# Splitting a softmax multiply over two engines and computing two feature blocks together in a kernel's opening

## The chip, the cores and the metric

The kernel runs on one core of a Trainium2 chip. A core has a matrix engine (TensorE, PE in the profile), VectorE (DVE), ScalarE (ACT), GpSimd (POOL) and SyncE (SP, which issues most DMAs). Each engine runs its own list of instructions in order and waits on semaphores for the others. The time is device microseconds of one execution. Before the change it is 418.26 us, the median of three runs (417.74 to 418.84).

## The reference, cut to what matters

Three layers on 4 batches of 576 tokens. The first compresses keys and values of each of 8 heads into 32 memory slots and attends to them; the second picks one of 8 experts per token, the third is a feed-forward layer with a convolution over the tokens:

```python
a   = softmax(phi)                                  # over the tokens' 32 slots
k_m = einsum('bhsm,bhsd->bhmd', a, k)
v_m = einsum('bhsm,bhsd->bhmd', a, v)               # V: 32 slots x 64 per head
s   = (q @ k_m.T) / sqrt(64);  e = exp(s - s.max(-1))
A   = e / (e.sum(-1) + 1e-9)                        # slot weights of each token
x   = A @ v_m                                       # 576 x 512 per batch
h   = relu(x @ w1[e]);  x = p[e] * (h @ w2[e])      # e: a token's expert
h   = relu(x @ w_in);   c = conv3(h) over tokens
out = (h * sigmoid(c)) @ w_out
```

## The kernel before, in words

The kernel never forms `A @ v_m` by itself. It multiplies V by the expert's first weights (V w1, 256 slot rows by 1024 features), and then h = relu(A · V w1), so that the tokens meet a matrix of 256 rows only. Every wide product is taken in a high and a low part, in the format `F32R`: ScalarE copies a float32 tile to its high part, VectorE subtracts that to get the low part, and TensorE runs three products (high·high, high·low, low·high) into one PSUM bank. This is `split` and `matmul3` (lines 145 to 160), and `vw_high` and `vw_low` for V w1.

A batch's tokens are taken in two halves of 288. The names in the profile: `sc` the scores in PSUM, `st` and `sd` the same with tokens down the partitions, `smx` the sums over slots, `at` the weights A with slots down the partitions again, `att` their high and low parts; `pv` the products V w1 in PSUM, `vh` and `vl` their high and low parts; `ph` the products A · V w1, `h` both parts of the relu; `wb` the split second weights w2, `py` the products h w2. `pa` are transposes of `ex`, the exponentials of phi, on TensorE; `nm` is the negative of phi's largest value, `rs` the sums. `idle` are products of the identity that nobody reads (`warm`, line 458).

The order of the work at the start is written by hand. `OPENING` (lines 40 to 48) is a list of steps; with it the order on TensorE, VectorE, ScalarE and SyncE is that of the list, so each of these engines gets its instructions of a step behind those of the step before. What follows the opening is laid out by a planner for TensorE alone, and by a scheduler for the others.

The steps that matter here: `ssum.0.0` (`slot_weights`, line 509) turns the exponentials of batch 0's first half into A; `ahi` and `alo` split it; `vwe`, `vwh`, `vwl` form the first two feature blocks of V w1; `vw.0.1` to `vw.0.3` the other three pairs; each `h.0` is one of eight feature blocks of h. `pmax.3`, `pexp.3` and `prec.3` are the softmax of phi's fourth tile, which `pback.3` transposes on TensorE. `w2part` splits half of the first piece of w2. For the first half alone, `slot_exp`, the sums and the transposes come in two pieces of 9 slot groups (`pieces`, line 483), but the multiply by the reciprocal is one instruction:

```python
nc.vector.tensor_tensor(by_slots(st), d3, of_heads(sm), ALU.mult)      # 128x576
```

Of the kernel before, what the change touches and what calls it, by code (L numbers as in the profile page):

```python
# [14 lines left out]
ALU = mybir.AluOpType  # L15
# [9 lines left out]
HALF = S // 2  # L25
# [15 lines left out]
phi.0 phi.1 kv.0 firstq.0 kv.1 gates phi.2 phi.3 q.0.0 firstq.1 kv.2 warm.0.8  # L41
pmax.0 pexp.0 pmax.1 pexp.1 prec.0 prec.1 pback.0 pback.1 mem.0.0 warm.0.1 mem.0.1 memf.0 warm.0.5 mem.1.0 warm.0.2 mem.1.1 memf.1
frow.0 pmax.2 fexp.0 warm.0.3 back.0 warm.1.2 gatew.0 flog.0 scores.0.0 pexp.2 pback.2
strn.0.0 smx.0.0 ssub.0.0 sexp.0.0 ssum.0.0 warm.1.8 mem.2.0 mem.2.1 warm.1.1 w1.0 q.0.1 wload.0.0 wload.0.1 kv.3 vwe.0 vwh.0 warm.1.2 vwe.1 ahi.0.0 vwh.1 alo.0.0 vwl.0 vwl.1 warm.1.3 wload.0.2
q.1.0 wload.0.3 q.1.1 cload nload.0 nload.1 phi.4 kv.4 prec.2 memf.2 pmax.3
h.0 vw.0.1 h.0 pexp.3 vw.0.2 h.0 prec.3 h.0 w2part.0 vw.0.3 h.0 scores.0.1 strn.0.1 w2part.1 h.0 pback.3 h.0 h.0 smx.0.1 w2.0.1 ssub.0.1 w2.0.2 sexp.0.1
y.0 firstq.2 phi.5 kv.5 mem.3 ssum.0.1 w2.0.3 y.0 back.1 ahi.0.1 alo.0.1 nar.0 nload.2 y.0 gatew.1 frow.1 fexp.1 nar.1 nload.3 y.0
""".split()

# [65 lines left out]
def fused_kernel(tc, q, first, first_q, kv, kv_tail, phi, w1, w2, w_in, conv_w, w_out, out):  # L115
    nc = tc.nc
    wide = w_in.dtype == I64
    PSUM = bass.MemoryType.PSUM
    with (
# [18 lines left out]
        def rows(g):  # L138

            return slice(64 * g, 64 * g + 64)  # L140

        def slots(h):

            return slice(32 * h, 32 * h + 32)
# [2 lines left out]
            pin(nc.scalar.activation(hi, src, AF.Copy))  # L147
            pin((eng or nc.vector).tensor_tensor(lo, src, hi.bitcast(F32), ALU.subtract))  # L148

        def matmul3(outs, pairs, pin=lambda ins: ins, low_last=False):  # L150


            terms = []
            for (sh, sl), (mh, ml) in pairs:
                terms += [(sh, mh), (sh, ml), (sl, mh)]
            if low_last:
                terms = [t for i in range(3) for t in terms[i::3]]
            for i, (st, mv) in enumerate(terms):
                for ps, cols in outs:
                    pin(nc.tensor.matmul(ps, st, mv[:, cols], start=i == 0, stop=i == len(terms) - 1))  # L160

        def urgent():

            return tc.high_priority(offset=1500)
# [7 lines left out]
        def half(i):  # L172
            return slice(i * HALF, (i + 1) * HALF)
# [336 lines left out]
        def slot_weights(b, hf):  # L510
            st, d3 = sts.pop((b, hf)), by_slots(sds.pop((b, hf)))
            sm = ap.tile([128, 18], F32, tag="smx", bufs=2, name=f"smx{b}_{hf}")
            for hs in pieces(b, hf):
                nc.vector.reduce_sum(sm[:, hs], d3[:, hs], axis=AX.X)
            nc.vector.tensor_scalar(sm, sm, EPS, None, ALU.add)
            nc.vector.reciprocal(sm, sm)
            nc.vector.tensor_tensor(by_slots(st), d3, of_heads(sm), ALU.mult)
            attf[b, hf] = ap.tile([128, 2, HALF], F32, tag="at", bufs=4, name=f"at{b}_{hf}")
            for hs in pieces(b, hf):
                cols = slice(32 * hs.start, 32 * hs.stop)  # L520
                nc.vector.transpose(attf[b, hf].rearrange("p g t -> p (g t)")[:, cols], st[:, cols])
# [6 lines left out]
        def slot_softmax(b, hf):  # L528

            slot_top(b, hf)  # L530
            slot_exp(b, hf)
            slot_weights(b, hf)
# [183 lines left out]
        att, e0 = {}, {}  # L716
# [10 lines left out]
        def vw_product(vs, raws, q, name, into=None):  # L727


            hi, lo = into or (fps[-1].tile([128, 4, 2, 128], F32R, tag="vw", bufs=4, name=f"{p}{name}_{q // 2}")  # L730
                              for p in ("vh", "vl"))
            ps = banks(f"pv{name}_{q}")
            at = q % 2
            for i, raw in enumerate(raws):
                fs = slice(2 * (at + i), 2 * (at + i) + 2)
                by_head(by_block(ps)[:, :, fs], lambda g, h: vs[rows(g), slots(h)], lambda g, h: by_block_head(raw)[rows(g), :, h])
            with urgent():
                fs = slice(2 * at, 2 * (at + len(raws)))
                vw_high(hi, ps, fs)
                vw_low(lo, hi, ps, fs)  # L740
            return hi, lo

        def by_block(ps):
            return ps.rearrange("p g (f n) -> p g f n", f=4)

        def by_block_head(raw):
            return raw.rearrange("p (f h n) -> p f h n", f=2, h=4)

        def vw_high(hi, ps, fs):
            nc.scalar.activation(hi[:, fs], ps.rearrange("p g (f n) -> p f g n", f=4)[:, fs], AF.Copy)  # L750

        def vw_low(lo, hi, ps, fs):
            nc.vector.tensor_tensor(lo[:, fs], ps.rearrange("p g (f n) -> p f g n", f=4)[:, fs],
                                    hi[:, fs].bitcast(F32), ALU.subtract)
# [17 lines left out]
        def hidden(vw, at, f, hf, name):  # L772

            ps = bank(f"ph{name}_{hf}{f}")[:, :HALF]
            hi, lo = vw[f // 4]
            matmul3([(ps, half(hf))],
                    [((hi[:, f % 4, g, :], lo[:, f % 4, g, :]), (at[:, g, 0, :], at[:, g, 1, :])) for g in range(2)],
                    low_last=f"{name}{hf}{f}" == "000")
            t = fps[-1].tile([128, 2, HALF], F32R, tag="h", bufs=8, name=f"h{name}_{hf}{f}")
            with urgent():  # L780
                nc.scalar.activation(t[:, 0, :], ps, AF.Relu)  # L781
                low = nc.vector.scalar_tensor_tensor(t[:, 1, :], ps, 0.0, t[:, 0, :].bitcast(F32), ALU.max, ALU.subtract)  # L782
                hidden_low.append(low.ins)
            return t

        def second(hs, wbb, d, name):
            ps = bank(f"py{name}_{d}")[:, :HALF]
            w = wbb[d].rearrange("p s (f d) -> p s f d", f=8)
            matmul3([(ps, slice(0, HALF))],
                    [((w[:, 0, f], w[:, 1, f]), (hs[f][:, 0, :], hs[f][:, 1, :])) for f in range(8)])  # L790
            return ps
# [14 lines left out]
        late, wbs, vws, wi, hids, count = [], {}, {}, {}, [], {}  # L806
# [93 lines left out]
        def load_first():  # L900
            ys0.append(load_y(0, expert(0)))

        def split_first():
            ys0.append(y_parts(0))
            split_y(0, ys0[0], *ys0[1])

        def gated_w(kc):
# [7 lines left out]
            "scores": scores, "gatew": gate_weights, "firstq": first_queries, "frow": first_row, "fexp": first_weights, "flog": first_expert, "ssoft": slot_softmax,  # L915
            "pmax": phi_max, "pexp": phi_exp, "prec": phi_sums, "smax": slot_top, "strn": scores_back, "smx": slot_max,
            "ssub": slot_difference, "sexp": slot_exp, "ssum": slot_weights, "ahi": attention_high, "alo": attention_low,
            "rtok": route_tokens, "save": save, "rback": route_back, "rall": route_all, "rpp": route_scan, "rown": route_first, "asplit": split_attention,
            "vwe": first_vw, "vwh": first_vw_high, "vwl": first_vw_low, "vw": expert_vw, "w2": expert_w2, "nload": load_words, "nar": narrow, "win": gated_w,
            "conv": conv_weights, "cload": load_conv, "w1": expert_w1, "w2part": first_w2, "wload": load_w2, "close": close, "yload": lambda b: load_first(), "ysplit": lambda b: split_first(), "h": next_hidden, "y": next_second,  # L920
        }

# [27 lines left out]
        def other_experts(b):  # L950
# [8 lines left out]
            with tc.For_i(0, E) as e:  # L959
                fl = nc.values_load(fli[0:1, ds(b * E + e, 1)], min_val=0, max_val=1)  # L960
                with tc.If(fl > 0):
# [188 lines left out]
```

## Time and profile before

The profiled execution took 417.01 us, 1.25 us less than the median above. Its span, from the first to the last instruction that the profile shows, is 415.2 us, so 1.8 us lie outside it.

| Engine | busy us | share of the span | instructions |
| --- | --- | --- | --- |
| PE (matmul) | 406.6 | 98% | 3406 |
| DVE | 276.3 | 67% | 509 |
| ACT | 222.0 | 53% | 414 |
| POOL | 74.6 | 18% | 121 |

The times of instructions are taken from the span's start. Busy time of TensorE includes the `idle` products, and a busy matrix engine is not one at its peak. The mean granted clock of the matrix engine was 0.997 of full speed. What the change touches lies between 16 and 32 us of the span.

### The profile page before, as it was taken

Reading aid. Unit: us, or ns where it says so; the run is one execution under the profiler, and the core shown is the slowest. Engines: PE = TensorE matmul, PEld = TensorE weight load, DVE = VectorE, ACT = ScalarE, POOL = GpSimd, SP = SyncE. Lnnn points to the kernel's source line nnn. Section 1 sums busy time; section 2 is a strip of 40 time slices with the busy share of each in tenths; the row PEclk is TensorE's granted clock in tenths of the full one; section 3 lists DMA queues with packets and bytes.
Section 4 is the critical chain, followed back from the end, with each engine's and each line's share of the span. In section 5 each row is a group of like instructions: output and inputs, shape, how many; then the busy total and the mean of one; then the engine's idle time right before and its main releaser. Section 6 shows DMA issues by size and latency. Waiting matters only on the chain.

```text
span 415.2 us, 8514 instructions
## 1 busy us (share of the span) xinstructions
PE 406.6 (98%) x3406; PEld 370.6 (89%) x3407; DVE 276.3 (67%) x509; ACT 222.0 (53%) x414; POOL 74.6 (18%) x121
## 2 busy tenths in 40 slices
PE   8999999999999999999999999999999999999994
PEld 7779988989989998899999988998889988999884
DVE  3689899695777974966979980688105792178500
ACT  4366577455657264645848742677215772277320
POOL 1000202311122211311101620034100332014300
PEclk9999999999999999999999999999999999999998
DMA  8999989967892699946640032000120000100022
GB/s 288 343 403 401 340 305 363 410 220 277 303 310 93 200 366 407 340 157 186 194 152 0 2 114 103 0 2 0 57 70 2 0 2 29 72 2 2 2 77 57
DMA packets 23904, 69.04 MB, mean 166 GB/s; under 512 B 3280, under 2 KB 4048, under 8 KB 23856
## 3 DMA queue, kind: packets, MB, share of 16 engines
q1 hardware_dynamic: 20272, 56.88, 39.1%
q0 software_dynamic: 3584, 11.54, 7.1%
q8 instruction: 28, 0.46, 0.5%
q14 instruction: 20, 0.16, 0.1%
HBM read 52.08 MB, written 16.33 MB: 165 GB/s over the span
## 4 chain that ended last, share of the span: by engine, by line
PE 96%; ACT 1%; DMA 1%; DVE 1%; issue 0%; ACTq 0%
PE py L160 25%; PE pi L160 24%; PE po L1058 24%; PE ph L160 12%; PE pv L455 2%; PE pk L412 2%; PE idle L462 2%; PE sc L455 1%; PE pa L390 1%; DMA ph<-in_phi 1%; PE pl L593 1%; PE pk L402 0%; DVE wb L148 0%; PE pkt L446 0%; ACT wb L147 0%
## 5 line engine op out<-in xcount | busy, mean ns | idle before, releaser
L160 PE MATMUL py<-h,wb 128*128 128x288 f32 x768 | 108.2, 298 | 0.0
L160 PEld LDWEIGHTS py<-h,wb 128*128 128x128 f32 x768 | 103.0, 188 | 4.2 <-issue 3.4
L160 PE MATMUL pi<-yh,wi 128*128 128x288 f32 x512 | 90.4, 295 | 0.0
L1058 PE MATMUL po<-wo,g 128*128 128x512 f32 (+1 forms) x408 | 90.2, 377 | 0.0
L1058 PEld LDWEIGHTS po<-wo,g 128*128 128x128 f32 x408 | 72.8, 188 | 13.2
L160 PEld LDWEIGHTS pi<-yh,wi 128*128 128x128 f32 x512 | 76.3, 188 | 0.9
L1040 DVE SCALAR_TENSOR_TENSOR ct<-ht,convw,ct 128x575 f32<-128x575 f32 x32 | 31.0, 968 | 52.1 <-ACT ct L1039 52.1
L160 PE MATMUL pi<-yl,wi 128*128 128x288 f32 x256 | 54.6, 295 | 0.0
L160 PE MATMUL ph<-att,vh 128*128 128x288 f32 x256 | 53.5, 302 | 0.3 <-DVE h L782 0.3
L1023 POOL CAST tail<-g 128x128 fp32r<-128x128 f32 x32 | 23.0, 723 | 122.9 <-DVE g L148 122.3
L160 PEld LDWEIGHTS ph<-att,vh 128*128 128x128 f32 x256 | 40.6, 188 | 4.6 <-DVE h L782 1.7
L865 POOL DMA_DIRECT2D ydram<-ys x32 | 17.4, 545 | 146.7 <-ACT ys L864 140.3
L160 PEld LDWEIGHTS pi<-yl,wi 128*128 128x128 f32 x256 | 41.1, 188 | 0.0
L1037 ACT ACTIVATE ht<-pi 128x576 f32<-128x576 f32 x32 | 20.8, 651 | 33.5 <-PE pi L160 33.5
L160 PE MATMUL ph<-att,vl 128*128 128x288 f32 x128 | 37.7, 296 | 0.0
L782 DVE SCALAR_TENSOR_TENSOR h<-ph,h 128x288 fp32r<-128x288 f32 x64 | 28.1, 449 | 12.8 <-ACT h L781 12.7
L781 ACT ACTIVATE h<-ph 128x288 fp32r<-128x288 f32 x64 | 25.7, 408 | 16.5 <-PE ph L160 16.1
L864 ACT ACTIVATE ys<-py 128x288 f32<-128x288 f32 x32 | 13.1, 408 | 37.5 <-PE py L160 25.2
L1082 ACT ACTIVATE ot<-po 128x512 f32<-128x512 f32 x17 | 9.5, 598 | 43.3 <-PE po L1058 43.3
L1018 DVE TENSOR_TENSOR ct<-ht,ct 128x576 f32<-128x576 f32 x32 | 27.0, 844 | 7.2 <-ACT ct L1017 7.1
L1042 DVE SCALAR_TENSOR_TENSOR ct<-ht,convw,ct 128x575 f32<-128x575 f32 x32 | 28.3, 886 | 0.4
L147 ACT ACTIVATE g<-ct 128x576 fp32r<-128x576 f32 x32 | 21.7, 681 | 12.6 <-DVE ct L1018 12.6
(234 smaller groups left out, 505.2 us busy)
## 6 DMA issues: line engine op xcount, KB each, us to landing
kv<-in_kv SPq DMA_DIRECT2D x16, 512.0 KB, 8.5
q<-in_q SPq DMA_DIRECT2D x8, 576.0 KB, 10.3
ydram<-ys POOLq DMA_DIRECT2D x32, 144.0 KB, 5.3
y<-ydram SPq DMA_DIRECT2D x4, 1152.0 KB, 6.8
out<-ot SPq DMA_DIRECT2D x15, 256.0 KB, 2.0
ph<-in_phi SPq DMA_DIRECT2D x8, 288.0 KB, 7.3
adram<-at POOLq DMA_DIRECT2D x8, 288.0 KB, 7.7
wa_1r<-in_w SPq DMA_DIRECT2D x4, 512.0 KB, 4.5
```

Source lines behind the costliest of these rows:

```text
L147: pin(nc.scalar.activation(hi, src, AF.Copy))
L160: pin(nc.tensor.matmul(ps, st, mv[:, cols], start=i == 0, stop=i == len(terms) - 1))
L781: nc.scalar.activation(t[:, 0, :], ps, AF.Relu)
L782: low = nc.vector.scalar_tensor_tensor(t[:, 1, :], ps, 0.0, t[:, 0, :].bitcast(F32), ALU.max, ALU.subtract)
L864: nc.scalar.activation(yt, ps, AF.Copy)
L865: stored.append(nc.gpsimd.dma_start(ydram[b, d, :, half(hf)], yt).ins)
L1018: slow(f"gm.{f}").tensor_tensor(ct, ht, ct, ALU.mult)
L1023: nc.gpsimd.tensor_copy(tail[:, f, :, to:to + 64], t[:, :, 512:576].bitcast(F32))
L1037: nc.scalar.activation(two(ht), halves(ps), AF.Relu)
L1040: nc.vector.scalar_tensor_tensor(ct[:, 1:], ht[:, :S - 1], convw[:, 0, f:f + 1], ct[:, 1:], ALU.mult, ALU.add)
L1042: nc.vector.scalar_tensor_tensor(ct[:, :S - 1], ht[:, 1:], convw[:, 2, f:f + 1], ct[:, :S - 1], ALU.mult, ALU.add)
L1058: nc.tensor.matmul(ps[:, cols], st[sp], w[:, mp, f % 2, cols], start=f == 0 and i == 0, stop=f == 7 and i == 2)
```

## The change: what it does

- The multiply in `slot_weights` of the first half becomes two of 128x288. GpSimd takes the second (slot groups 9 to 17), VectorE the first.
- Of the 14 `idle` products between `pa` of phi's third tile and h, 8 stay: 5 behind `pa` and 3 between the two feature blocks of `pv_0`.
- The first two feature blocks of h are computed together. `hp` issues the eight products with the high part of V w1 for both, `hq` behind `vw.0.1` the four with the low part and then both relus. Before, block 0 stood ahead of `vw.0.1` (with its low products last, by `low_last`) and block 1 behind it.
- The split of `vw.0.1` into high and low parts is done in two pieces of 128x256.
- `pmax.3` and `pexp.3` move from in front of the first `h.0` and from behind the second to behind the fourth, ahead of `w2part.0`; `prec.3` moves from behind the third `h.0` to behind the fifth.

```diff
-strn.0.0 smx.0.0 ssub.0.0 sexp.0.0 ssum.0.0 warm.1.8 mem.2.0 mem.2.1 warm.1.1 w1.0 ... vwe.0 vwh.0 warm.1.2 vwe.1 ahi.0.0 vwh.1 alo.0.0 vwl.0 vwl.1 warm.1.3 wload.0.2
-q.1.0 wload.0.3 q.1.1 cload nload.0 nload.1 phi.4 kv.4 prec.2 memf.2 pmax.3
-h.0 vw.0.1 h.0 pexp.3 vw.0.2 h.0 prec.3 h.0 w2part.0 vw.0.3 h.0 scores.0.1 strn.0.1 w2part.1 h.0 pback.3 h.0 h.0 ...
+strn.0.0 smx.0.0 ssub.0.0 sexp.0.0 ssum.0.0 warm.1.5 mem.2.0 mem.2.1 w1.0 ... vwe.0 vwh.0 warm.1.3 vwe.1 ahi.0.0 vwh.1 alo.0.0 vwl.0 vwl.1 wload.0.2
+q.1.0 wload.0.3 q.1.1 cload nload.0 nload.1 phi.4 kv.4
+hp.0 prec.2 memf.2 vw.0.1 hq.0 h.0 vw.0.2 h.0 pmax.3 pexp.3 w2part.0 vw.0.3 h.0 prec.3 scores.0.1 strn.0.1 w2part.1 h.0 pback.3 h.0 h.0 ...
...
-            nc.vector.tensor_tensor(by_slots(st), d3, of_heads(sm), ALU.mult)
             attf[b, hf] = ap.tile([128, 2, HALF], F32, tag="at", bufs=4, name=f"at{b}_{hf}")
+            for hs in pieces(b, hf)[::-1]:
+                (nc.gpsimd if 0 < hs.start else nc.vector).tensor_tensor(
+                    by_slots(st)[:, hs], d3[:, hs], of_heads(sm[:, hs]), ALU.mult)
...
                 fs = slice(2 * at, 2 * (at + len(raws)))
-                vw_high(hi, ps, fs)
-                vw_low(lo, hi, ps, fs)
+                for part in [slice(f, f + 1) for f in (2, 3)] if (name, q) == ("0", 1) else [fs]:
+                    vw_high(hi, ps, part)
+                for part in [slice(f, f + 1) for f in (2, 3)] if (name, q) == ("0", 1) else [fs]:
+                    vw_low(lo, hi, ps, part)
...
+        def first_hidden(low):
...
+            for i, (st, mv) in enumerate([(1, 0)] if low else [(0, 0), (0, 1)]):
+                for f in range(2):
+                    for g in range(2):
+                        nc.tensor.matmul(first_ps[f], vw[st][:, f, g, :], at[:, g, mv, :HALF],
+                                         start=not low and i == g == 0, stop=low and g == 1)
+            if low:
+                count["h"] = 1
+                hids.extend(hidden_out(first_ps[f], f, 0, "0") for f in range(2))
```

`hidden_out` holds the two instructions of the relu (lines 781 and 782 of before) that stood in `hidden`.

On TensorE, from the last `idle` products to `pv_2` (`att` is A split, the number behind a name tells tiles apart). Before:

```order
L462 MATMUL idle_275<-ident 128x128 x2
L455 MATMUL pv_0_394<-wa_0r,vt_273 32x128 x8
L462 MATMUL idle_275<-ident 128x128 x3
L160 MATMUL ph_00_454<-att_414,vh_0_392 128x288 x4
L160 MATMUL ph_00_454<-att_414,vl_0_393 128x288 x2
L455 MATMUL pv_1_464<-wa_1r,vt_273 32x256 x8
L160 MATMUL ph_01_475<-att_414,vh_0_392 128x288 x2
L160 MATMUL ph_01_475<-att_414,vl_0_393 128x288
L160 MATMUL ph_01_475<-att_414,vh_0_392 128x288 x2
L160 MATMUL ph_01_475<-att_414,vl_0_393 128x288
L455 MATMUL pv_2_490<-wa_2r,vt_273 32x256 x8
```

And now:

```order
L460 MATMUL idle_275<-ident 128x128 x3
L453 MATMUL pv_0_391<-wa_0r,vt_273 32x128 x8
L798 MATMUL ph_00_440<-att_412,vh_0_389 128x288 x2
L798 MATMUL ph_01_441<-att_412,vh_0_389 128x288 x2
L798 MATMUL ph_00_440<-att_412,vh_0_389 128x288 x2
L798 MATMUL ph_01_441<-att_412,vh_0_389 128x288 x2
L453 MATMUL pv_1_457<-wa_1r,vt_273 32x256 x8
L798 MATMUL ph_00_440<-att_412,vl_0_390 128x288 x2
L798 MATMUL ph_01_441<-att_412,vl_0_390 128x288 x2
L158 MATMUL ph_02_480<-att_412,vh_0_389 128x288 x2
```

The products with `vl` of blocks 0 and 1 now stand behind `pv_1`, and three `idle` products in front of `ph_00` are gone.

On ScalarE, from the split of `pv_1` to the relu of block 4 (`h_04`); `ex` from `ph_143` is `pexp.3`, the half piece of `wb_0` is `w2part.0`. Before:

```order
L750 ACTIVATE vh_0_392<-pv_1_464 128x512
L781 ACTIVATE h_01_482<-ph_01_475 128x288
L369 ACTIVATE ex_485,rs_486<-ph_143,nm_452 128x576
L750 ACTIVATE vh_1_488<-pv_2_490 128x512
L781 ACTIVATE h_02_508<-ph_02_501 128x288
L781 ACTIVATE h_03_522<-ph_03_515 128x288
L147 ACTIVATE wb_0_525<-wb_0r 128x512
L750 ACTIVATE vh_1_488<-pv_3_528 128x512
L781 ACTIVATE h_04_546<-ph_04_539 128x288
```

And now:

```order
L752 ACTIVATE vh_0_389<-pv_1_457 128x256 x2
L785 ACTIVATE h_00_474<-ph_00_440 128x288
L785 ACTIVATE h_01_477<-ph_01_441 128x288
L785 ACTIVATE h_02_487<-ph_02_480 128x288
L752 ACTIVATE vh_1_490<-pv_2_492 128x512
L785 ACTIVATE h_03_510<-ph_03_503 128x288
L367 ACTIVATE ex_515,rs_516<-ph_143,nm_513 128x576
L147 ACTIVATE wb_0_518<-wb_0r 128x512
L752 ACTIVATE vh_1_490<-pv_3_521 128x512
L785 ACTIVATE h_04_539<-ph_04_532 128x288
```

The exponential went from in front of block 2's relu (`h_02`) to between block 3's (`h_03`) and `wb_0`.

On VectorE, over the same steps (`nm` is `pmax.3`, `rs` with `nm`'s `ex` is `prec.3`). Before:

```order
L364 TENSOR_REDUCE nm_452<-ph_143 128x1
L782 SCALAR_TENSOR_TENSOR h_00_461<-ph_00_454,h_00_461 128x288
L753 TENSOR_TENSOR vl_0_393<-pv_1_464,vh_0_392 128x512
L782 SCALAR_TENSOR_TENSOR h_01_482<-ph_01_475,h_01_482 128x288
L753 TENSOR_TENSOR vl_1_489<-pv_2_490,vh_1_488 128x512
L782 SCALAR_TENSOR_TENSOR h_02_508<-ph_02_501,h_02_508 128x288
L372 TENSOR_SCALAR rs_486<-rs_486 128x1
L373 RECIPROCAL rs_486<-rs_486 128x1
L375 TENSOR_SCALAR rs_513<-rs_486 128x1
L782 SCALAR_TENSOR_TENSOR h_03_522<-ph_03_515,h_03_522 128x288
L148 TENSOR_TENSOR wb_0_525<-wb_0r,wb_0_525 128x512
L753 TENSOR_TENSOR vl_1_489<-pv_3_528,vh_1_488 128x512
L782 SCALAR_TENSOR_TENSOR h_04_546<-ph_04_539,h_04_546 128x288
```

And now:

```order
L755 TENSOR_TENSOR vl_0_390<-pv_1_457,vh_0_389 128x256 x2
L786 SCALAR_TENSOR_TENSOR h_00_474<-ph_00_440,h_00_474 128x288
L786 SCALAR_TENSOR_TENSOR h_01_477<-ph_01_441,h_01_477 128x288
L786 SCALAR_TENSOR_TENSOR h_02_487<-ph_02_480,h_02_487 128x288
L755 TENSOR_TENSOR vl_1_491<-pv_2_492,vh_1_490 128x512
L786 SCALAR_TENSOR_TENSOR h_03_510<-ph_03_503,h_03_510 128x288
L362 TENSOR_REDUCE nm_513<-ph_143 128x1
L148 TENSOR_TENSOR wb_0_518<-wb_0r,wb_0_518 128x512
L755 TENSOR_TENSOR vl_1_491<-pv_3_521,vh_1_490 128x512
L786 SCALAR_TENSOR_TENSOR h_04_539<-ph_04_532,h_04_539 128x288
```

The reduction of `ph_143`, which `ex` needs, now stands behind the low part of block 3 and in front of `wb_0` and the last `vl`.

On TensorE nothing changes place from block 2 to `py`. The new kernel's rows from the second half's scores (`sc_1`) to block 6 (`ph_06`), with the engine that an instruction waits for:

```order
L453 MATMUL sc_1_546<-q_1_380,vt_273 32x288 [waits DMAHW5_49,PE_49]
L453 MATMUL sc_1_546<-q_1_380,vt_273 32x288 x7
L158 MATMUL ph_05_559<-att_412,vh_1_490 128x288 x2
L158 MATMUL ph_05_559<-att_412,vl_1_491 128x288
L158 MATMUL ph_05_559<-att_412,vh_1_490 128x288 x2
L158 MATMUL ph_05_559<-att_412,vl_1_491 128x288
L388 MATMUL pa_569<-ident,ex_515 128x128 [waits DVE_49]
L388 MATMUL pa_569<-ident,ex_515 128x128 x3
L390 MATMUL pa_569<-ident,ex_515 128x128
L158 MATMUL ph_06_578<-att_412,vh_1_490 128x288 [waits Activation_49]
L158 MATMUL ph_06_578<-att_412,vh_1_490 128x288
```

Here the transposes `pa` stand behind block 5 in both kernels, and their first instruction waits for VectorE: for the last `vl`, which empties the PSUM banks of `pv_3` that `pa` takes over.

## Rows read from the trace of the kernel before

**Rows 1.** Page part 4: the chain that ended last, shares by engine.

```profile
PE 96%; ACT 1%; DMA 1%; DVE 1%; issue 0%; ACTq 0%
```

**Rows 2.** Chain of waits, 16 to 34 us: start us, us, what.

```profile
16.48 1.79 PE idle L462 x16
...
19.62 0.42 PE idle L462 x2
...
20.42 0.64 PE idle L462 x4
...
21.44 0.86 PE idle L462 x6
22.31 1.05 PE ph L160 x6
23.36 0.59 PE pv L455 x16
23.95 0.98 PE ph L160 x6
...
25.52 1.91 PE ph L160 x12
```

**Rows 3.** VectorE in order of time: start, us, line, out<-in [idle before].

```profile
19.53 0.27 DVE L516 RECIPROCAL smx<-smx 128x18 f32<-128x18 f32 x1
19.83 0.76 DVE L517 TENSOR_TENSOR st<-sd,smx 128x576 f32<-128x576 f32 x1
20.62 0.84 DVE L521 STREAM_TRANSPOSE at<-st 128x288 f32<-128x288 f32 x2
...
22.35 0.75 DVE L753 TENSOR_TENSOR vl<-pv,vh 128x256 fp32r<-128x256 f32 x2
...
23.58 0.28 DVE L435 SCALAR_TENSOR_TENSOR q0r<-pk,rs,q0r 128x64 f32<-128x64 f32 x1
...
23.79 0.75 DVE L364 TENSOR_REDUCE nm<-ph 128x1 f32<-128x576 f32 x1
...
28.07 0.45 DVE L782 SCALAR_TENSOR_TENSOR h<-ph,h 128x288 fp32r<-128x288 f32 x1
29.07 0.69 DVE L148 TENSOR_TENSOR wb<-wb_0r,wb 128x512 fp32r<-128x512 f32 x1 [0.55 <-ACT wb L147]
29.68 0.68 DVE L753 TENSOR_TENSOR vl<-pv,vh 128x512 fp32r<-128x512 f32 x1
```

**Rows 4.** ScalarE in order of time, the same stretch.

```profile
21.84 0.36 ACT L750 ACTIVATE vh<-pv 128x256 fp32r<-128x256 f32 x1
23.91 0.37 ACT L437 ACTIVATE pm<-pk,rs 128x128 f32<-128x128 f32 x1 [1.70 <-DVE q0r L435]
...
25.27 0.77 ACT L369 ACTIVATE ex<-ph,nm 128x576 f32<-128x576 f32 x1
...
27.47 0.41 ACT L781 ACTIVATE h<-ph 128x288 fp32r<-128x288 f32 x1 [0.38 <-PE ph L160]
28.41 0.63 ACT L147 ACTIVATE wb<-wb_0r 128x512 fp32r<-128x512 f32 x1 [0.53 <-DMA wb_0r<-in_w]
28.94 0.58 ACT L750 ACTIVATE vh<-pv 128x512 fp32r<-128x512 f32 x1
```

**Rows 5.** TensorE in order of time: the transposes of ex.3.

```profile
30.48 0.60 PE L390 MATMUL pa<-ident,ex 128*128 128x128 f32 x4
```

**Rows 6.** VectorE in order of time, 241 to 245 us.

```profile
241.52 0.81 DVE L1040 SCALAR_TENSOR_TENSOR ct<-ht,convw,ct 128x575 f32<-128x575 f32 x1
242.37 2.07 DVE L1042 SCALAR_TENSOR_TENSOR ct<-ht,convw,ct 128x575 f32<-128x575 f32 x1
```

**Rows 7.** GpSimd in order of time, the same stretch.

```profile
242.40 1.42 POOL L148 TENSOR_TENSOR g<-ct,g 128x576 fp32r<-128x576 f32 x1 [4.23 <-ACT g L147]
```

**Rows 8.** Stretches: us, busy us of each engine (instructions), PEclk, DMA, GB/s.

```profile
174.00:175.20 1.20, 0.86 (x7) 0.62 (x6) 1.20 (x5) 0.79 (x2) 0.00 (x0) 1.00 1.00 409
...
409.00:415.20 6.20, 0.23 (x2) 0.03 (x1) 0.00 (x0) 0.38 (x1) 0.00 (x0) 0.79 0.09 29
```

More of the change, by code (lines that the diff above doesn't have):

```diff
@@ L43 @@
 frow.0 pmax.2 fexp.0 warm.0.3 back.0 warm.1.2 gatew.0 flog.0 scores.0.0 pexp.2 pback.2
-strn.0.0 smx.0.0 ssub.0.0 sexp.0.0 ssum.0.0 warm.1.8 mem.2.0 mem.2.1 warm.1.1 w1.0 q.0.1 wload.0.0 wload.0.1 kv.3 vwe.0 vwh.0 warm.1.2 vwe.1 ahi.0.0 vwh.1 alo.0.0 vwl.0 vwl.1 warm.1.3 wload.0.2
-q.1.0 wload.0.3 q.1.1 cload nload.0 nload.1 phi.4 kv.4 prec.2 memf.2 pmax.3
-h.0 vw.0.1 h.0 pexp.3 vw.0.2 h.0 prec.3 h.0 w2part.0 vw.0.3 h.0 scores.0.1 strn.0.1 w2part.1 h.0 pback.3 h.0 h.0 smx.0.1 w2.0.1 ssub.0.1 w2.0.2 sexp.0.1
+strn.0.0 smx.0.0 ssub.0.0 sexp.0.0 ssum.0.0 warm.1.5 mem.2.0 mem.2.1 w1.0 q.0.1 wload.0.0 wload.0.1 kv.3 vwe.0 vwh.0 warm.1.3 vwe.1 ahi.0.0 vwh.1 alo.0.0 vwl.0 vwl.1 wload.0.2
+q.1.0 wload.0.3 q.1.1 cload nload.0 nload.1 phi.4 kv.4
+hp.0 prec.2 memf.2 vw.0.1 hq.0 h.0 vw.0.2 h.0 pmax.3 pexp.3 w2part.0 vw.0.3 h.0 prec.3 scores.0.1 strn.0.1 w2part.1 h.0 pback.3 h.0 h.0 smx.0.1 w2.0.1 ssub.0.1 w2.0.2 sexp.0.1
 y.0 firstq.2 phi.5 kv.5 mem.3 ssum.0.1 w2.0.3 y.0 back.1 ahi.0.1 alo.0.1 nar.0 nload.2 y.0 gatew.1 frow.1 fexp.1 nar.1 nload.3 y.0
@@ L148, in split, with matmul3 @@
             pin((eng or nc.vector).tensor_tensor(lo, src, hi.bitcast(F32), ALU.subtract))
-        def matmul3(outs, pairs, pin=lambda ins: ins, low_last=False):
+        def matmul3(outs, pairs, pin=lambda ins: ins):
             terms = []
@@ L155, in matmul3 @@
                 terms += [(sh, mh), (sh, ml), (sl, mh)]
-            if low_last:
-                terms = [t for i in range(3) for t in terms[i::3]]
             for i, (st, mv) in enumerate(terms):
@@ L776, in hidden, with hidden_out @@
             matmul3([(ps, half(hf))],
-                    [((hi[:, f % 4, g, :], lo[:, f % 4, g, :]), (at[:, g, 0, :], at[:, g, 1, :])) for g in range(2)],
-                    low_last=f"{name}{hf}{f}" == "000")
+                    [((hi[:, f % 4, g, :], lo[:, f % 4, g, :]), (at[:, g, 0, :], at[:, g, 1, :])) for g in range(2)])
+            return hidden_out(ps, f, hf, name)
+        def hidden_out(ps, f, hf, name):
             t = fps[-1].tile([128, 2, HALF], F32R, tag="h", bufs=8, name=f"h{name}_{hf}{f}")
@@ L784, in hidden @@
             return t
+        def first_hidden(low):
+            vw, at = vws[0][0], att[0]
+            if not low:
+                first_ps.extend(bank(f"ph0_0{f}")[:, :HALF] for f in range(2))
+            for i, (st, mv) in enumerate([(1, 0)] if low else [(0, 0), (0, 1)]):
[6 more added lines that the diff above has]
+                hids.extend(hidden_out(first_ps[f], f, 0, "0") for f in range(2))
+        first_ps = []
         def second(hs, wbb, d, name):
@@ L918, in fused_kernel @@
             "rtok": route_tokens, "save": save, "rback": route_back, "rall": route_all, "rpp": route_scan, "rown": route_first, "asplit": split_attention,
-            "vwe": first_vw, "vwh": first_vw_high, "vwl": first_vw_low, "vw": expert_vw, "w2": expert_w2, "nload": load_words, "nar": narrow, "win": gated_w,
+            "hp": lambda b: first_hidden(False), "hq": lambda b: first_hidden(True), "vwe": first_vw, "vwh": first_vw_high, "vwl": first_vw_low, "vw": expert_vw, "w2": expert_w2, "nload": load_words, "nar": narrow, "win": gated_w,
             "conv": conv_weights, "cload": load_conv, "w1": expert_w1, "w2part": first_w2, "wload": load_w2, "close": close, "yload": lambda b: load_first(), "ysplit": lambda b: split_first(), "h": next_hidden, "y": next_second,
```

## The prediction, made before the changed kernel ran

> **What bounds the kernel now.** I read the shares of the chain that ended last first. TensorE holds 96% of it and no other engine more than 1% [rows 1], so a change counts only by what it does to TensorE's own row of work: products taken out of it, or gaps put in. Next I read the chain between 16 and 34 us, where everything moved lies [rows 2]. It never leaves TensorE there. But four of its pieces are `idle` products, which stand where the engine would otherwise wait: 1.79 + 0.42 + 0.64 + 0.86 = 3.71 us. So the stretch before h is bound by what the idle products cover, the making of A on VectorE and ScalarE. Then come the three lists of instructions in order of time. VectorE works without a gap from the reciprocal at 19.53 to 23.8 [rows 3]; ScalarE waits for its results [rows 4]. Behind them TensorE runs densely to `pa` at 30.48 [rows 5], which waits for VectorE's last `vl`. That `vl` ran from 29.68 to 30.36 [rows 3], so it is ready about when TensorE arrives, with no slack to spend. Work of block 3 of h ends on TensorE at T = 25.52 + 1.91 = 27.43 [rows 2]; from there to `pa` it has 30.48 − 27.43 = 3.05 us of work (`pv_3`, block 4, scores, block 5). The change leaves that list alone.
>
> **Part 1: fewer idle products.** Fourteen become eight (each has two records). At the old rates 5 of the first 8 take 1.12 us and 3 of the last kind 0.86, 1.98 in all, so 1.73 us of products go. I cost this at nothing: they covered waits for A's high part and for `vh`, whose times don't hang on them. TensorE just waits instead.
>
> **Part 2: the multiply split over two engines.** Now it takes 0.76 us, 19.83 to 20.59, and the transposes start at 20.62 [rows 3]. If nothing collided, VectorE's half would take 0.38, and GpSimd's second half 0.71 to 0.75, half of the 1.42 that a 128x576 multiply took there [rows 7]; the second transpose could go about 0.4 us earlier. But both engines read the same two tiles at the same time, and at 242 us the trace has such a pair. A GpSimd multiply ran 242.40 to 243.82, its normal 1.42 [rows 7], and the VectorE instruction of 242.37 beside it took 2.07 us, where its twin just before took 0.81 [rows 6]. It ended at 244.44, 0.62 behind GpSimd: VectorE stood still and then did most of its work. The same here: the reciprocal ends at 19.80, GpSimd works 19.87 to 20.62, and VectorE's half ends 0.38 × 0.62 / 0.81 = 0.29 later, at 20.91. The transposes start at 20.93 in place of 20.62: **+0.31 us** for all that hangs on A. The ends for GpSimd's half are 0.71 (no cost per instruction) and 1.42 (all of it), so the term lies between −0.4, without a collision, and +1.0. I take +0.31, from the one pair of rows that shows both engines on such work.
>
> The Trainium skill ("SBUF — State Buffer", section "SBUF: two separate sides") has a rule for such a pair: the two engines share a port pair as an exclusive lock, and whichever starts first holds it for its whole instruction. The trace agrees that one stands still (2.07 against 0.81 us), but there the engine that lost had started 0.03 us before the other. By the rule VectorE, which starts at 19.83, goes first and GpSimd follows to about 20.95; the multiply would then cost the second transpose little, which is the second case below.
>
> **Part 3: two blocks of h together, the split of `vw.0.1` in two.** The first of these products needs A's high part and `vh`. The second `vh` ends at 21.84 + 0.36 = 22.20 [rows 4], and by +0.31 at 22.51. TensorE issues block 1's high products from 22.56; the six products from there take 0.98, as six do between two `pv` [rows 2], to 23.54. `pv_1` takes 0.59 [rows 2], to 24.13, and the four low ones 4 × 0.16 = 0.64 (12 products took 1.91 [rows 2]), to 24.77. Here something new is late. Block 2 needs `vw.0.1` split. ScalarE must first do `pm`, which waits for `q0r`: 23.58 + 0.28 + 0.31 = 24.17, so `pm` runs 24.22 to 24.59 [rows 3, 4]. Then come two `vh` of 0.36 with about 0.28 between their starts, 24.51 to 25.15. VectorE's first `vl` waits for both, 25.18 to 25.59 (half of the pair's 0.75 and the overlap [rows 3]). Block 2's third product takes that `vl` at 25.62; its last four products end at 26.26. `pv_2` 0.59, block 3 0.98: T = 27.83, against 27.43. **+0.40 us** at the end of block 3, 0.09 of it from the new order itself. Block 0 no longer waits for the first `vl` pair ahead of `pv_1`; this wait stands in its place.
>
> **Part 4: `pmax.3` and `pexp.3` moved behind block 3.** This is where I see most of the cost. Before, the reduction ran at 23.79 and `ex` at 25.27 [rows 3, 4], while TensorE was busy elsewhere, and ScalarE idled 0.53 us for `wb_0r` from memory ahead of its 28.41 [rows 4]. Now both stand in the chain that `pa` waits for. In order: block 3 ends at T; relu on ScalarE T+0.04, 0.41 [rows 4], ends T+0.45; low part on VectorE 0.03 later, 0.45 [rows 3], ends T+0.93; `nm` 0.08 before that end (instructions overlap so much in these rows), 0.75 [rows 3], ends T+1.60; `ex` 0.05 later, 0.77 [rows 4], ends T+2.42; `wb_0`'s high part 0.63 [rows 4] to T+3.05, with `wb_0r` long there; its low part starts T+3.08, the last `vl` 0.61 behind it (29.07 to 29.68), 0.68 [rows 3], ends T+4.37; `pa` some 0.03 later, at T+4.40. TensorE arrives at T+3.05. A new wait of **1.35 us**, where before there was almost none. `prec.3` is moved behind the low part of block 4, and nobody waits for it (its user, `pm` of the fourth tile, comes after `pa`).
>
> **Sum.** `pa` starts 0.40 + 1.35 = 1.75 us later. From `pa` on TensorE has dense work of the same order in both kernels, so this passes to the end: 417.01 + 1.75 = 418.76 against the profiled execution of 417.01, and 418.26 + 1.75 = **420.0 us** against the median. The removed products return none of it.
>
> **Rivals.**
> - *VectorE goes first in the multiply.* Against: the rows of part 2. For: it is ready 0.04 to 0.07 earlier than I put GpSimd's start. Then part 2 costs near nothing and T shifts by 0.09: 0.09 + 1.35 = 1.44, 419.7 us. By the Trainium skill's rule of part 2 this is what happens.
> - *The transfer of `wb_0r` already delays `pa` in the runs that are timed.* The median lies 1.25 us above the profiled execution, and in that one ScalarE already waited for this transfer [rows 4]. If it lands 1 us later than 28.41 there, the old kernel stalls at `pa` by about as much, and the new one, which needs it only at T+2.42 = 30.25, does not. The cost is then 1.75 less about 1: 418.9 us. Against: nothing says that the 1.25 us lie here.
> - *Not slower: VectorE's last `vl` doesn't hold `pa`.* One place and one price: if the chain behind block 3 is done by T+3.05, as when the reduction and `ex` start on their own inputs instead of behind block 3's relu, part 4 is free. `nm` would have to run 1.35 us earlier, in VectorE's gaps at block 2. With A's transposes 0.4 us earlier (part 2 without a collision) the time falls by about 0.6 at most, 417.7 us. Against: each engine takes its instructions in the list's order, and the list has the reduction behind block 3's low part.
> - *The clock.* The row of 409 to 415 us shows a granted clock of 0.79 behind a TensorE that had almost stopped (0.23 us busy of 6.20), and at 174 us a gap of 0.34 in 1.20 left it at 1.00 [rows 8]. If a wait of 1.35 us at `pa` dropped it from 2.4 to 1.2 GHz, the next products run at half speed: the 12 of blocks 6 and 7 take 1.91 us now [rows 2] and would take that much more, with as many of `py` 3.8 us, so 422 to 424 us. The gap is nearer to 174's, so I give it little.
>
> **How the numbers follow.** My forecast 0.42, VectorE first 0.24, the late transfer 0.20, not slower 0.09, the clock 0.05. The two first together give 419.7 to 420.0; with the bounds of part 2 (T from −0.25 to +1.1) they reach from 1.1 to 2.5 us over the median, 419.4 to 420.8. The range of 8 in 10 takes in the late transfer downward and a little of the clock upward: 418.2 to 421.3. What this kernel's measurement tells from no change is about 0.3%, 1.25 us. Slower by more: most of the forecast (0.38), half of VectorE first (0.13), the clock (0.05): 0.56. Within: the late transfer (0.19), the rest of those two (0.15), half of not slower: 0.38. Faster by more: 0.06, if part 2's full gain and no wait at `pa` come together.
>
> **What would show it.** Right: in the profile after, `pa` of the fourth tile starts near 32.2 and 1.3 us behind the last product of block 5, with the wait put down to `vl`; `ex` runs just ahead of `wb_0` near 29.5; GpSimd's multiply takes about 0.75 and VectorE's half beside it about 1.0; the first transpose starts near 20.9. Wrong: `pa` within 0.3 us of block 5's end; a VectorE half of 0.4 us; a gap in front of block 2 well over 0.7 us or none; a PEclk under 1.00 behind `pa`. If the time is under 418, the transfer or the order of the engines was not what I read.

## The result and the profile after

The changed kernel took 420.82 us, the median of 21 runs (419.30 to 424.15), against 418.69 us of the kernel before, measured anew beside it (21 runs, 417.74 to 420.82). The ratio is 1.0058 with an interval of [1.0041, 1.0074]: slower by 0.6%, where I forecast 420.0 us in 418.2 to 421.3. The profiled execution took 421.19 us, its span 419.4.

The page's shares of the chain that ended last, now:

```profile
PE 90%; DMA 3%; DVE 3%; ACT 2%; issue 0%; SPq 0%; POOL 0%; ACTq 0%; POOLq 0%
```

Against [rows 1] TensorE gave up 6 points to transfers, VectorE and ScalarE: the chain now leaves it. The points of the transfers aren't the change's own: these pieces are a `kv` at the start and one at 62 to 69 us, both told below. The chain of waits from block 3 of h to `pa` (start us, us, what):

```profile
27.50 1.00 PE ph L158 x6
28.52 0.42 ACT h L785
...
28.97 0.46 DVE h L786
29.42 0.67 DVE nm L362
...
30.12 0.87 ACT ex L367 x2
30.99 0.53 ACT wb L147
...
31.55 0.69 DVE wb L148
32.24 0.61 DVE vl L755
32.85 0.04 issue
32.89 0.66 PE pa L388 x4
```

It is the chain that the prediction built link by link. Block 3 ends at 28.48 (its last product 28.19 + 0.29), `pa` starts at 32.89, so 4.41 us later; forecast were 4.40. In [rows 2, 5] this was 3.05. TensorE in order of time says how long it stood:

```profile
31.39 0.30 PE L158 MATMUL ph<-att,vl 128*128 128x288 f32 x1
32.89 0.66 PE L388 MATMUL pa<-ident,ex 128*128 128x128 f32 x4 [1.20 <-DVE vl L755]
```

The bracket is the wait and who ended it: 1.20 us for the last `vl`. Where there is no wait an instruction starts about 0.16 before its predecessor's end, so `pa` came 1.36 us late (4.41 − 3.05).

The multiply of A. VectorE and GpSimd in order of time:

```profile
20.43 0.27 DVE L514 RECIPROCAL smx<-smx 128x18 f32<-128x18 f32 x1
20.73 0.46 DVE L517 TENSOR_TENSOR st<-sd,smx 128x288 f32<-128x288 f32 x1
21.23 1.01 DVE L521 STREAM_TRANSPOSE at<-st 128x288 f32<-128x288 f32 x2
```

```profile
20.85 0.87 POOL L517 TENSOR_TENSOR st<-sd,smx 128x288 f32<-128x288 f32 x1 [18.80 <-DVE smx L514]
```

VectorE went first and was not held up: 0.46 us, not 1.0. The second transpose waits for GpSimd and ends 1.54 us behind the reciprocal (22.24 − 20.70), where before both ended 1.66 behind it ([rows 3]: 21.46 − 19.80). The split saves 0.12 us.

Two more pieces of the 4.2 us between the two spans lie outside all this. The reciprocal itself came 0.90 us later than in [rows 3], a shift from before anything that the change touches: the second `kv` landed at 9.00 us and TensorE waited for it.

```profile
9.05 0.65 PE L410 MATMUL pk<-kv,a 128*32 128x128 f32 x16 [0.85 <-DMA kv<-in_kv]
```

And at 69 us ScalarE waited for the next expert's `wb_0r`, with TensorE behind it:

```profile
68.27 1.06 ACT L147 ACTIVATE wb<-wb_0r 128x1024 fp32r<-128x1024 f32 x1 [2.10 <-DMA wb_0r<-in_w]
```

```profile
70.77 0.26 PE L453 MATMUL pw<-wgl,vt 64*32 64x9 f32 x13 [1.61 <-ACT vt L446]
```

So of 4.2 us, 0.90 is a late `kv`, 0.15 the front of the change (block 3 ends 7.79 behind the reciprocal, before 7.64), 1.36 the wait at `pa`, 1.61 a late transfer at 69 us; 0.2 lie in smaller pieces. Whether the two transfers belong to the change only more kernels could say.

### The profile page after: what moved, and what is told of

Same layout as the page of the kernel before. It is cut to its first block, busy times and chain, and to the rows that moved or that the text cites. A ratio compares the mean times of both kernels' runs of the same rounds, so it can differ in the third digit from the quotient of the medians.

```text
span 419.4 us, 8495 instructions
## 1 busy us (share of the span) xinstructions
PE 406.2 (97%) x3394; PEld 369.0 (88%) x3395; DVE 276.2 (66%) x510; ACT 222.1 (53%) x415; POOL 75.6 (18%) x122
## 4 chain that ended last, share of the span: by engine, by line
PE 90%; DMA 3%; DVE 3%; ACT 2%; issue 0%; SPq 0%; POOL 0%; ACTq 0%; POOLq 0%
PE pi L158 24%; PE py L158 24%; PE po L1078 23%; PE ph L158 11%; DMA q<-in_q 2%; DMA kv<-in_kv 2%; PE pv L453 2%; PE pk L410 2%; PE sc L453 1%; PE idle L460 1%; PE pa L388 1%; PE pl L593 1%; DVE wb L148 0%; DVE vl L755 0%; PE pk L400 0%; ACT wb L147 0%
## 5 line engine op out<-in xcount | busy, mean ns | idle before, releaser
L158 PE MATMUL ph<-att,vh 128*128 128x288 f32 x248 | 52.0, 302 | 0.3 <-DVE h L786 0.3
L158 PEld LDWEIGHTS ph<-att,vh 128*128 128x128 f32 x248 | 39.3, 188 | 4.5 <-DVE h L786 1.9
L158 PE MATMUL ph<-att,vl 128*128 128x288 f32 x124 | 36.6, 295 | 0.2 <-DVE vl L755 0.2
```

## The experiments

All kernels that follow are read by the same four marks, taken from the reciprocal of the slot sums (R) so that a late transfer at the start doesn't count: R itself, the end of block 3 behind R, the start of `pa` behind block 3, and the rest of the span (spans are known to 0.1 us). The ratio is that of the times to the kernel before on the same chip.

| kernel | R | block 3 − R | pa − block 3 | span − pa | ratio [interval] |
| --- | --- | --- | --- | --- | --- |
| before | 19.79 | 7.64 | 3.05 | 384.72 | 1 |
| changed | 20.70 | 7.79 | 4.41 | 386.51 | 1.0058 [1.0041, 1.0074] |
| e1 early exponential | 20.79 | 8.21 | 3.05 | 385.15 | 0.9997 [0.9979, 1.0015] |
| e2 late exponential only | 20.40 | 8.43 | 4.40 | 385.07 | 1.0036 [1.0020, 1.0051] |
| e3 VectorE only | 20.27 | 8.05 | 4.40 | 384.88 | 1.0047 [1.0030, 1.0064] |
| e4 split only | 21.56 | 8.17 | 3.16 | 388.71 | 1.0046 [1.0017, 1.0075] |
| e5 e1 with old idle | 23.93 | 7.82 | 3.55 | 385.19 | 0.9998 [0.9978, 1.0017] |
| e6 delay by idle | 21.40 | 7.72 | 4.38 | 385.40 | 1.0019 [0.9997, 1.0040] |
| e7 split again | 21.10 | 7.50 | 3.51 | 384.89 | 0.9990 [0.9966, 1.0013] |
| e8 e1, VectorE only | 23.95 | 10.17 | 3.04 | 385.24 | 1.0002 [0.9981, 1.0024] |
| e9 changed again | 21.23 | 7.77 | 4.40 | 384.80 | 1.0024 [1.0004, 1.0044] |
| e10 w2 behind | 21.34 | 8.38 | 3.76 | 386.42 | 1.0031 [1.0018, 1.0043] |
| e11 late exponential again | 21.29 | 7.68 | 4.40 | 384.93 | 1.0011 [0.9997, 1.0026] |
| e12 early exponential again | 20.35 | 7.78 | 3.05 | 384.93 | 1.0002 [0.9984, 1.0020] |

Where block 3 ends more than 8 us behind R, TensorE waited for `wa_1r` in front of `pv_1`: 0.51 us in e1, 0.84 in e2, 0.21 in e3, 0.72 in e4, 0.70 in e10 and 1.42 in e8. That transfer is no part of the change. With the late exponential the rest of the span is never shorter than in the kernel before, so nothing of the wait at `pa` is given back behind it.

**Putting the exponential back.** The changed kernel with one line of the list edited:

```diff
-hp.0 prec.2 memf.2 vw.0.1 hq.0 h.0 vw.0.2 h.0 pmax.3 pexp.3 w2part.0 vw.0.3 h.0 prec.3 ...
+hp.0 prec.2 memf.2 pmax.3 vw.0.1 hq.0 pexp.3 h.0 vw.0.2 h.0 w2part.0 vw.0.3 h.0 prec.3 ...
```

> The changed kernel with the reduction and the exponential of phi's fourth tile put back early: the reduction behind the reciprocal of the third tile's sums and ahead of the split of vw.0.1, the exponential behind the relus of blocks 0 and 1; nothing else differs from the changed kernel. Theory (their new place holds up the transposes pa): the wait of 1.20 us ahead of pa goes, block 3 still ends some 0.15 us later than in the kernel before (counted from the reciprocal of the slot sums), and the time is 0 to 0.4 us above the kernel before: ratio 1.000 to 1.001 to the kernel before. Rival (the cost lies in the new order of blocks 0 and 1 or in the transfer at 69 us, and the wait at pa is given back later anyway): the time stays 1.5 to 2.5 us above the kernel before, ratio 1.004 to 1.006.

Measured 0.9997. TensorE reaches `pa` and goes on, with no bracket in its row:

```profile
32.05 0.60 PE L388 MATMUL pa<-ident,ex 128*128 128x128 f32 x4
```

All of the loss is gone, with every other part of the change in place. Run again with the changed kernel beside it (same edit):

> The kernel of e1_early_exp again (the changed kernel with the early exponential), beside the changed kernel: ratio 0.999 to 1.001 to the kernel before. If the rest of the change has a cost of its own that the first run missed: 1.001 to 1.003.

Measured 1.0002. Its block 3 ends 0.14 us later than before, `pa` 3.05 behind.

**The late exponential alone.** The kernel before, with the list edited to the new places:

```diff
-... nload.0 nload.1 phi.4 kv.4 prec.2 memf.2 pmax.3
-h.0 vw.0.1 h.0 pexp.3 vw.0.2 h.0 prec.3 h.0 w2part.0 vw.0.3 h.0 scores.0.1 ...
+... nload.0 nload.1 phi.4 kv.4 prec.2 memf.2
+h.0 vw.0.1 h.0 vw.0.2 h.0 h.0 pmax.3 pexp.3 w2part.0 vw.0.3 h.0 prec.3 scores.0.1 ...
```

> The kernel before with one part of the change alone: the reduction, the exponential and the sums of phi's fourth tile moved to where the changed kernel has them. Theory: pa waits for VectorE's last vl some 4.4 us behind the end of block 3, a stall of 1.2 to 1.4 us, and the time is 1.2 to 1.5 us above the kernel before: ratio about 1.003. If transfers at 69 us are then late too, as in the profile of the changed kernel, up to 1 us more, 1.005. Rival (the move costs nothing by itself): ratio 1.000.

Measured 1.0036, 1.5 us, with the forecast row:

```profile
33.23 0.66 PE L390 MATMUL pa<-ident,ex 128*128 128x128 f32 x4 [1.19 <-DVE vl L753]
```

> The kernel of e2_late_exp_only again (the kernel before with the late exponential alone), beside the changed kernel: 1.2 to 1.6 us above the kernel before, ratio 1.003 to 1.004, if the wait at pa is worth what it measures; 1.005 to 1.006 if a late pa draws a second cost.

Again the same wait (1.20), but a ratio of 1.0011 only, below both expectations; the interval reaches to 1.0026, 1.1 us, so not up to the wait. The row is the same in each profile, the time of a set of runs is not: it moves by 0.2% from one set to the next. Over the five sets with the whole chain (changed, e2, e3, e9, e11) the mean of the ratios is 1.0035, 1.5 us.

**The multiply on VectorE.** The changed kernel with the one 128x576 instruction:

```diff
-            for hs in pieces(b, hf)[::-1]:
-                (nc.gpsimd if 0 < hs.start else nc.vector).tensor_tensor(
-                    by_slots(st)[:, hs], d3[:, hs], of_heads(sm[:, hs]), ALU.mult)
+            nc.vector.tensor_tensor(by_slots(st), d3, of_heads(sm), ALU.mult)
```

> The changed kernel with the multiply of A as one instruction of 128x576 on VectorE again, the rest as changed. Theory (the two engines hardly hinder each other, 0.46 and 0.87 us beside each other in the profile of the changed kernel): transposes start 20.62 less 20.33, so 0.29 us later behind the reciprocal than with the split, but end only 0.1 us later; time 0 to 0.2 us above the changed kernel, ratio to the kernel before 1.005 to 1.006. My forecast's collision (the split costs 0.31 us): time 0.3 us below the changed kernel, ratio 1.004 to 1.005.

Measured 1.0047 from six runs, which tells the two expectations apart no further; the profile does: the second transpose ends 1.67 us behind R, 0.13 later than with the split. The wait at `pa` is 1.20 again.

**The split alone.** The kernel before with the reverse of that edit:

> The kernel before with the multiply split over VectorE and GpSimd alone. Theory (VectorE first, GpSimd beside it 0.87 us): the second transpose ends 0.1 us earlier, the idle products in front of the first ph keep TensorE anyway, so ratio 1.000 (0.9995 to 1.0003). Forecast's collision: all that hangs on A is 0.31 us later, ratio 1.0007; the profile tells the two apart by VectorE's half, 0.46 us or about 1.0.

VectorE's half took 0.46 and GpSimd's 0.87, so the collision is refuted. But the ratio was 1.0046, from times in two groups. So it was run again, unchanged:

> The same kernel as e4_split_only, run again, since its times fell into two groups, 418.0 to 420.7 and 422.6 to 423.9 us, where its profile in the opening shows nothing that costs. If the split itself costs: ratio 1.003 to 1.006 again, with some times above 422. If the groups were those of that chip at that time: ratio 1.000 to 1.001 and no times above 421.

Measured 0.9990. The groups didn't come back, though one time of 421.59 is above the 421 that was named. The first profile is of an execution of the upper group (423.42 us), and it shows what that one holds: 2.06 us of wait at 69 us, for `wb_0r` as in the changed kernel, and behind it a lower granted clock (third number from the end), which cost another 1.5 us (the shift against the kernel before is 4.91 behind the wait, at 71.26, and 6.43 at 77.23):

```profile
69.00:72.00 3.00, 0.94 (x34) 0.54 (x40) 2.15 (x3) 3.00 (x6) 0.21 (x1) 0.85 0.77 296
72.00:76.00 4.00, 4.00 (x47) 2.98 (x28) 4.00 (x9) 2.35 (x6) 0.33 (x1) 0.68 0.99 354
```

The second shows my rival of the late transfer in the opening, where ScalarE stands for the first `wb_0r`:

```profile
30.10 0.63 ACT L147 ACTIVATE wb<-wb_0r 128x512 fp32r<-128x512 f32 x1 [1.05 <-DMA wb_0r<-in_w]
```

It landed near 30.1, and `pa` waited 0.30 us for it without any move of the exponential. In such an execution the late exponential costs that much less.

**The idle products.** e1 with all fourteen idle products at their old places:

```diff
-... ssum.0.0 warm.1.5 mem.2.0 mem.2.1 w1.0 ... vwh.0 warm.1.3 vwe.1 ... vwl.0 vwl.1 wload.0.2
+... ssum.0.0 warm.1.8 mem.2.0 mem.2.1 warm.1.1 w1.0 ... vwh.0 warm.1.2 vwe.1 ... vwl.0 vwl.1 warm.1.3 wload.0.2
```

> The changed kernel with the reduction and the exponential put back early, as in e1_early_exp, and with all fourteen idle products back at their old places. Theory (idle products only fill waits): the time is that of e1_early_exp, ratio 0.999 to 1.001 to the kernel before, and block 3 of h ends within 0.3 us of e1_early_exp's, counted from the reciprocal of the slot sums. Rival (fewer idle products free TensorE for real work): 0.3 to 1.7 us slower than e1_early_exp, ratio 1.001 to 1.004.

Measured 0.9998: six idle products more or less are worth nothing that the interval, 0.8 us to either side, would show, and block 3 ends 7.82 behind R against 7.78 in e12. Its `pa` is 0.50 late because of the first `wb_0r`, as in e7. Its profile shows something else too, told below.

**The delay alone.** The kernel before with idle products in front of `pa`:

```diff
-... strn.0.1 w2part.1 h.0 pback.3 h.0 h.0 ...
+... strn.0.1 w2part.1 h.0 warm.1.6 pback.3 h.0 h.0 ...
```

> The kernel before with six more idle products (about 1.34 us) in front of the transposes pa of phi's fourth tile, and nothing else: a delay of TensorE at the place where the changed kernel waits, without any move on the other engines. Theory (a wait at pa passes one to one to the end): 1.2 to 1.5 us above the kernel before, ratio 1.003. Rival (a delay here also makes the transfers of the next batch's weights late at 69 us, which is why the changed kernel is 2.4 us slower and not 1.5): 2 to 3 us, ratio 1.005 to 1.007. Rival (later stages give it back): ratio 1.000 to 1.001.

```profile
32.16 1.50 PE L462 MATMUL idle<-ident 128*128 128x128 f32 x12
33.50 0.60 PE L390 MATMUL pa<-ident,ex 128*128 128x128 f32 x4
```

`pa` 4.38 behind block 3, 1.33 late; measured 1.0019, about 0.8 us by the ratio and 1.1 by the medians, with an interval up to 1.7 us. It fits a loss passed on whole, and speaks against a second cost drawn by a late `pa`; it doesn't exclude that some is given back.

**Without the split, early.** e1 and e3 together:

> The changed kernel with the exponential put back early and the multiply on VectorE alone; so of the change there stay the new order of blocks 0 and 1, the halved split of vw.0.1 and the eight idle products. Theory: pa 3.05 us behind block 3, no wait there; block 3 ends 0.1 us later than with the split; the time is that of the kernel before, ratio 0.999 to 1.001. If the split costs in transfers later on, this kernel is faster than e1_early_exp by up to 1 us: ratio 0.997 to 0.999.

Measured 1.0002. The new order of blocks 0 and 1, by itself, moves nothing that the interval would show.

**A shorter chain.** If `pa` waits for this chain, taking one link out shortens the wait by that link:

```diff
-... pmax.3 pexp.3 w2part.0 vw.0.3 h.0 prec.3 ...
+... pmax.3 pexp.3 vw.0.3 w2part.0 h.0 prec.3 ...
```

> The changed kernel with the half split of w2's first piece (w2part.0) moved from in front of vw.0.3 to behind it; the exponential stays late. The chain that pa waits for loses wb's 0.63 us on ScalarE (0.03 less): it becomes relu, low part, reduction, exponential to T+2.42, vh 0.58, vl from T+3.03 to 3.71, so pa at about T+3.75 and a wait of 0.55 us in place of 1.20. Theory: 0.6 to 0.7 us less than the changed kernel, ratio 1.0015 to 1.0025 if pa is the only cost. Rival (pa waits for the exponential itself or for something else than this chain): pa stays at T+4.4 and the time that of the changed kernel.

The chain of waits from block 3 on:

```profile
28.74 0.99 PE ph L158 x6
...
29.75 0.42 ACT h L785
...
30.20 0.46 DVE h L786
30.66 0.67 DVE nm L362
...
31.35 0.87 ACT ex L367 x2
32.22 0.49 ACT vh L752
...
32.73 0.70 DVE vl L755
33.44 0.04 issue
33.48 0.66 PE pa L388 x4
```

`pa` 3.76 behind block 3 and a wait of 0.56, within a hundredth of what was expected; `wb` is out of the chain. In time it doesn't show: 1.0031, no less than the 1.0024 of the changed kernel in the same set (below), the interval [1.0018, 1.0043] holding the expected 1.0015 to 1.0025 only in part. This profile has a wait of 1.55 us at 69 us too.

**The changed kernel again.**

> The changed kernel, run again beside the three others of this group, because its 2.4 us over the kernel before are about 0.9 more than the 1.5 us that its opening shows. If only the wait at pa costs: ratio 1.003 to 1.004, the same as the late exponential alone. If the changed kernel has a second cost: ratio 1.005 to 1.006 again, above the late exponential alone.

Measured 1.0024 [1.0004, 1.0044], with the same 1.20 us at `pa` and no wait at 69 us: below both expectations, nearer to that of the wait alone. The first set gave 1.0058. Over the six sets of kernels with the late exponential the ratios run from 1.0011 to 1.0058; over the six with an early one, without e6's added delay, from 0.9990 to 1.0002, and 1.0046 in e4's first set.

## Why the prediction was right

**The bound and the place: right.** The loss is the wait at `pa`, by the chain that was worked out: 4.41 us measured, 4.40 forecast. It appears in each profile with the late exponential, shrinks by one link when one is taken out, and is gone when the exponential goes back, with the time. That the time itself came within 0.8 us of 420.0 is in part luck: the sum held a delay of 0.31 that didn't occur, and the first set 0.6 us (by the medians) to 0.9 (by the ratio) that no term of it names.

**Part 2: the step that failed is the collision.** "GpSimd works 19.87 to 20.62, and VectorE's half ends 0.38 × 0.62 / 0.81 = 0.29 later": it took the pair of [rows 6, 7] as a pattern, in which GpSimd won although it started 0.03 us later. Here VectorE starts 0.12 us ahead (20.73 and 20.85) and isn't hindered: 0.46 us, where the subtraction `sd` of the same 128x288 took 0.45 at 18.77. In place of +0.31 the term is −0.12. So the rival "VectorE goes first" came true: it puts 1.44 us on the opening, my forecast 1.75, and 1.51 were measured. A VectorE half of 0.4 us was among the prediction's own signs of being wrong.

The pair was also not the only one, as the prediction has it. The trace of before has twelve such multiplies on GpSimd beside VectorE, and one shows the other outcome:

```profile
231.75 1.88 DVE L1042 SCALAR_TENSOR_TENSOR ct<-ht,convw,ct 128x575 f32<-128x575 f32 x1
```

```profile
232.97 1.96 POOL L148 TENSOR_TENSOR g<-ct,g 128x576 fp32r<-128x576 f32 x1
```

VectorE started 1.2 us ahead, and the multiply took 1.96 in place of 1.42. In all 14 traces VectorE lost where it was 0.03 to 0.04 us ahead (the place of [rows 6, 7]); in the eight with the split it won 0.12 ahead. Where it turns was not measured, and the instructions differ.

GpSimd's half took 0.87 where half of 1.42 is 0.71, so 0.16 of it may be waiting. What the Trainium skill says ("SBUF — State Buffer", section "SBUF: two separate sides", whichever starts first holds the shared ports) fits here better than my row did; by its rule GpSimd would have stood until VectorE's end at 21.19, and 21.19 + 0.71 is 21.90, where it ended at 21.72. But the multiply of 232.97 too ended 0.12 sooner (234.93) than VectorE's end at 233.63 and its own 1.42 add up to. With as much taken off, an estimate for a half that stood is 21.78, so 21.72 doesn't speak against it. An undisturbed 0.87 isn't excluded either: no run has this half alone.

**Part 3: near in size, by two errors that cancel.** Block 3 ended 0.15 us late behind the reciprocal, and without the collision the forecast was 0.09. But the split brought `q0r`, the first link to block 2, 0.13 nearer to the reciprocal (24.35 − 20.70 = 3.65, in [rows 3] 23.58 − 19.80 = 3.78), which the 0.09 doesn't hold, and the four products behind the halved `vl` took 0.80 in the chain of waits where 4 × 0.16 = 0.64 was put. Block 2's wait for that `vl` is there, 0.20 us:

```profile
26.11 0.40 PE L158 MATMUL ph<-att,vl 128*128 128x288 f32 x1 [0.20 <-DVE vl L755]
```

```profile
26.11 0.80 PE ph L158 x4
```

**Part 1: right.** e5 shows no difference clear of the scatter.

**The rivals.** The clock: the granted clock stayed at 1.00 over the wait at `pa`:

```profile
31.00:34.00 3.00, 1.80 (x15) 1.57 (x14) 2.39 (x7) 2.35 (x6) 0.00 (x0) 1.00 1.04 410
```

The late transfer is real and not rare: in three of the seven profiles with an early exponential and no added delay (e4, e5, e7) the first `wb_0r` put `pa` 0.11, 0.50 and 0.46 us late. There the late exponential costs that much less, which may be why e11 measured so little; that was not shown. Not slower: excluded by the wait at `pa`, and by e1 and e2 together.

**What stays open.** The terms shown make 1.36 + 0.15 = 1.5 us, near e2 (1.5) and inside e9's interval (0.2 to 1.8 us); the first set's 2.4 us by the ratio exceeds them by 0.9. The wait at 69 us would fill it: 1.61, 2.06, 1.55, 0.47 and 0.30 us in the profiles of the changed kernel, e4, e10, e1 and e6, none in the other nine, the changed kernel's second profile and the kernel before among them. It comes with and without the late exponential. The three long ones are all in kernels with the split, e6's 0.30 alone is without; but four other profiles with the split have none. Seven of the first set's 21 executions took 422.17 us or more, where the kernel before stayed under 420.9; they may hold such a wait and a lower clock behind it, as in e4, but none of them was profiled. That a slip of the second expert's weights is likelier in one kernel than in another was not shown.

## What to carry to other kernels

When a step is moved out of the way of one consumer, walk the engine's list from its new place: everything queued behind it, and whoever waits for the last of that, pays for the move. Here a softmax nobody was in a hurry for was put ahead of a PSUM bank's release that TensorE needed at once. A multiply shared with GpSimd lasts as long as GpSimd's half: 0.87 us, more than the 0.76 of the whole on VectorE, and the gain was 0.12. And idle products that cover a wait are no reserve: taking them out gives nothing until the wait itself is shorter.

## What the runs showed of the hardware

The scatter between executions, which was larger than the effect, is in the profiles partly TensorE's clock after a late first transfer. In e5's profile TensorE stood 1.72 us for the first `kv` ahead of 8.66, and the rows of the next stretches read (us, busy us of PE, PEld, DVE, ACT, POOL, granted clock, DMA share, GB/s):

```profile
4.00:8.00 4.00, 2.69 (x17) 1.99 (x15) 2.06 (x8) 3.34 (x8) 0.00 (x0) 1.00 0.91 329
8.00:12.00 4.00, 3.34 (x50) 1.98 (x50) 0.00 (x0) 0.00 (x0) 0.00 (x0) 0.54 1.04 407
12.00:16.00 4.00, 4.00 (x42) 3.35 (x34) 0.29 (x2) 0.37 (x1) 0.00 (x0) 0.61 1.03 363
16.00:20.00 4.00, 3.56 (x66) 2.45 (x66) 2.56 (x13) 2.14 (x7) 0.00 (x0) 1.00 0.37 142
```

A granted clock near 0.5 is the lower of the two levels, 1.2 of 2.4 GHz. The transfer alone cost 1.3 us there, the clock another 2.8: the shift against the kernel before grew from 1.32 at 8.66 (before 7.34) to 4.14 at 15.97 (before 11.83), with no wait over 0.25 us between. In e8 the same happened behind 1.63 us, and once more behind a wait of 1.42 us for `wa_1r` at 27.5 (0.60 over 28 to 32 us). In e4 it stayed at 1.00 over 8 to 16 us behind a wait of 1.56 for the first `kv`, and fell behind 2.06 at 69 us. Behind the wait of 1.20 us at `pa` it stayed at 1.00 in all five profiles, so the length of a wait alone doesn't tell what follows.
